# A gated mix of linear attention and a ReLU layer: weight loads merged, value tiles moved forward, the last two tiles split in halves

## The chip, the cores and the metric

The kernel runs on one core of a Trainium2 chip. The core has several engines that run their own instruction queues and wait for one another by semaphores: TensorE (PE: matmuls, and PEld: the load of the stationary operand), VectorE (DVE), ScalarE (ACT), GpSimd (POOL) and SyncE (SP), which here only issues DMAs. The metric is the device time of one execution in microseconds (us); the figure given is the median of several runs.

## The reference, cut to what matters

Sizes: 2048 tokens, D = 512, 32 heads of 16 columns, a hidden layer of 1376 columns, all in bf16. Two branches read the same x and are mixed by a gate per token.

```python
g = sigmoid((x * gate_w).sum(-1, keepdims=True))
q, k, v = heads(x @ wqkv)                      # 32 heads of 16
pq, pk  = q @ w_phi[h], k @ w_phi[h]           # 16 x 16 per head
phi     = lambda t: concat(softmax(t), softmax(-t))
kv, z   = sum_s phi(pk) v, sum_s phi(pk)       # over all tokens
o       = (phi(pq) @ kv) / (phi(pq) . z + 1e-6)
a       = o @ wo
b       = relu(x @ w1) @ w2
out     = g * a + (1 - g) * b
```

## The kernel before, in words

The instructions of each engine are recorded by hand in the order in which the program is written: p.op adds one to an engine's queue with the events it waits for, p.dma does the same for a DMA, and emit turns events into semaphore waits. So the order of the source is the order of each queue. An engine takes its instructions strictly in order: one that waits holds up all that follow.

Tokens are worked on in 16 tiles of 128 (index m) and 4 chunks of 512 (index c). x is kept transposed in XT. The accumulators of TensorE are the 8 banks of PS. `free[bank]` names the event (an eviction by ScalarE or VectorE) after which a bank may be written again.

The stages, in order:

- **Loads** (L164 to L189, on SyncE): W1 in pieces, part of x, the rest of W1, w_phi, the value weights WV, then two transposing loads of the query and the key columns of wqkv (L185) into WQKT (a corner of PHQ), then chunks 1 to 3 of x, transposing (L188).
- **Slabs** (L518): eight 128-column blocks of the hidden layer for chunk 0, contraction slab by contraction slab; slab 3 waits for the load of W1's fourth row block (w13). Then hidden units (0, 8) and (0, 9), which also need the right-hand columns of W1.
- **Value tiles** (vtile, L401 to L414): four matmuls x @ wv into a bank (2, unless another is named), copied out to VS.
- **Folds** (pre, L300 to L313): the query and key weights are multiplied with w_phi, so that pq and pk come from x in one matmul. Eight of them, 0 to 3 for the query, 4 to 7 for the key; four matmuls each into banks 0, 1, 6, 7 in turn; even ones are copied out by VectorE, odd ones by ScalarE. Only 15 of 16 columns a head are computed, the 16th being a constant.
- **Ragged unit** (rest, L279 to L297): the last 96 columns of the hidden layer and the gate column for one chunk, token-major, evicted by two ScalarE instructions and transposed by a DMA.
- **The loop over tiles** (L574): atile(m) computes pq and pk of tile m (8 matmuls into banks 0 and 1), takes exponentials of both signs on ScalarE (two instructions over both banks, or four where m is in split), then the key chain (sum on VectorE, reciprocal, scaling into EB slot 3, on GpSimd except for tile 15) and the query chain (qchain, ending in a transposing DMA to PHQ). Behind atile(m) stand kv(m - 3), which adds tile m - 3 to the accumulators of kv in banks 6 and 7, vtile(m + 3), and the hidden units listed in mid[m] (hunit, L269: four matmuls and a relu eviction on ScalarE).
- **Hand-over** (L589 on): the remaining hidden units in late, with kv(13), kv(14), kv(15) and kvfin (VectorE masks kv into KVNZ) between them, then nd(0), qchain(15), the gate, finB(0, 4).
- **The output stage** (L608): per tile nd (phi(pq) @ kv, into banks 0 and 1 or 2 and 3), finB (hidden layer @ w2, eleven matmuls at L483), finA (@ wo), and comb, which mixes and stores.

Hidden units, ragged units and one value tile take their bank from a rotation over banks 3, 4 and 5:

```python
def nextbank():
    rot[0] += 1
    return 3 + (rot[0] - 1) % 3
```

finB(0, 4) names bank 4, and its first matmul waits for whatever eviction last freed that bank.

Of the kernel before, what the change touches and what calls it, by code (L numbers as in the profile page):

```python
# [68 lines left out]
def bass_gated_mix__linear_kernel_hedgehog__dense_activation_relu__prompt_kernel(  # L69
# [13 lines left out]
    S, D = x2.shape  # L83
# [3 lines left out]
    P = 128  # L87
# [17 lines left out]
    with ExitStack() as es:  # L105
# [55 lines left out]
        def loadw1(t, c0=0, c1=DFF, tag=""):  # L161
            p.dma("sp", lambda e: e.dma_start(  # L162
                out=W1[:, t, c0:c1], in_=B_w1[t * P:(t + 1) * P, c0:c1]), f"w1{t}{tag}", ev=f"w1{t}{tag}")
# [6 lines left out]
        p.early("sp")  # L170
        loadw1(0, 0, 4 * P, "a")
        loadw1(0, 4 * P, 8 * P)
        for t in (1, 2):
            loadw1(t, 0, 8 * P)
        p.dma("sp", lambda e: e.dma_start_transpose(  # L175
            out=XT[:, 2:4, 0:512], in_=x2[0:512, 2 * P:4 * P]), "x0t", ev="x0t")
        loadw1(3, 0, 8 * P)
        p.dma("sp", lambda e: e.dma_start(
            out=W1[:, :, 8 * P:DFF], in_=B_w1[:, 8 * P:DFF].rearrange("(j p) n -> p j n", p=P)), "w1r", ev="w1r")
        p.dma("sp", lambda e: e.dma_start(  # L180
            out=WPS[:, :, :], in_=A_w_phi.rearrange("(g hl) r c -> (hl r) g c", g=NDT)), "wps", ev="wps")
        p.dma("sp", lambda e: e.dma_start(  # L182
            out=WV[:, :, :], in_=A_wqkv[:, 2 * D:3 * D].rearrange("(j p) n -> p j n", p=P)), "wv", ev="wv")
        for i in range(2):
            p.dma("sp", lambda e, i=i: e.dma_start_transpose(  # L185
                out=WQKT[:, 4 * i:4 * i + 4, :], in_=A_wqkv[:, i * D:(i + 1) * D]), f"wqk{i}", ev=f"wqk{i}")
        for c in range(1, NCH):
            p.dma("sp", lambda e, c=c: e.dma_start_transpose(  # L188
                out=XT[:, :, c * 512:(c + 1) * 512], in_=x2[c * 512:(c + 1) * 512, :]), f"x{c}", ev=f"x{c}")  # L189
# [75 lines left out]
# [3 lines that stand above are left out]
# [32 lines left out]
        def pre(i):  # L300
            which, dt = i // 4, i % 4
            bank = (0, 1, 6, 7)[i % 4]
            dst = WQK[:, which, dt * DE:(dt + 1) * DE]
            after = [f"wqk{which}"] + [f"wbd{g}" for g in range(NDT)] + free[bank]
            for gt in range(NDT):
                p.op("pe", lambda e, gt=gt: e.matmul(  # L306
                    PS[:, bank, gt * 8 * FE:(gt + 1) * 8 * FE], WQKT[:, which * NDT + gt, dt * P:(dt + 1) * P],
                    Wbd[:, gt, :], start=True, stop=True),
                    after=(after if gt == 0 else ()), ev=(f"pm{i}" if gt == NDT - 1 else None))
            if i % 2 == 0:  # L310
                p.op("dve", lambda e: e.tensor_copy(dst, PS[:, bank, 0:DE]), after=[f"pm{i}"], ev=f"pc{i}")
            else:
                p.op("act", lambda e: e.activation(dst, PS[:, bank, 0:DE], ACT.Copy),  # L313
                     after=[f"pm{i}"], ev=f"pc{i}")
            free[bank] = [f"pc{i}"]

        split = (5, 8, 11, 13, 14, 15)

        def atile(m):
            b = m % NB  # L320
            first = xready(m // 4)
            order = [(dt, w) for dt in range(NDT) for w in range(2)]
            if m - 1 in split:
                order = [(dt, w) for w in (1, 0) for dt in range(NDT)]
            if m == 0:
                order = [(dt, w) for w in (0, 1) for dt in range(NDT)]
            for i, (dt, which) in enumerate(order):
                p.op("pe", lambda e, dt=dt, which=which: e.matmul(  # L328
                    PS[:, which, 0:DE], XT[:, dt, m * P:(m + 1) * P], WQK[:, which, dt * DE:(dt + 1) * DE],
                    start=(dt == 0), stop=(dt == NDT - 1)),  # L330
                    after=(first if i == 0 else []) + (free[which] if dt == 0 else [])
                    + ([f"pc{4 * which + c}" for c in range(4)] if m == 0 and dt == 0 else []),
                    ev=(f"qk{m}" if i == 7 else None))
            src = PS[:, 0:2, 0:DE].rearrange("p a (h f) -> p a h f", h=H)
            base = b * 8 * D
            busy = [f"tq{m - NB}", f"pk{m - NB}", f"pq{m - NB}"] if m >= NB else []

            def expo(s, w, ev):
                step = (4 * D, 2 * D)[s]
                off = base + s * (2 * D + 16)  # L340
                scale = (1.0, -1.0)[s]
                if w is None:
                    dst = bass.AP(tensor=EB, offset=off, ap=[[EBS, P], [step, 2], [32, H], [1, FE]])
                    s_ = src
                else:
                    dst = bass.AP(tensor=EB, offset=off + w * step, ap=[[EBS, P], [32, H], [1, FE]])
                    s_ = src[:, w, :, :]
                p.op("act", lambda e: e.activation(dst, s_, ACT.Exp, scale=scale),  # L348
                     after=[f"qk{m}"] + busy, ev=ev)

            if m in split:
                for w, nm in ((1, "k"), (0, "")):
                    expo(0, w, f"ep{nm}{m}")
                    expo(1, w, f"em{nm}{m}")
            else:
                expo(0, None, f"ep{m}")
                expo(1, None, f"em{m}")
            emk = f"emk{m}" if m in split else f"em{m}"
            free[1] = [emk]
            free[0] = [f"em{m}"]  # L360
            zk = ZB[:, b, 64:128].rearrange("p (h s) -> p h s", s=2)
            ek = EB[:, b, 2, :].rearrange("p (h s f) -> p h s f", h=H, s=2)
            if m == NT - 1:
                for s, nm in ((0, "epk"), (1, "emk")):
                    p.op("dve", lambda e, s=s: e.tensor_reduce(zk[:, :, s], ek[:, :, s, :], AX.X, ALU.add),
                         after=[f"{nm}{m}", f"cst{b}"], ev=f"zk{m}" if s else None)
            else:
                p.op("dve", lambda e: e.tensor_reduce(zk, ek, AX.X, ALU.add),  # L368
                     after=[emk, f"cst{b}"], ev=f"zk{m}")
            p.op("dve", lambda e: e.reciprocal(SC[:, b, 64:128], ZB[:, b, 64:128]),  # L370
                 after=[f"zk{m}"] + ([f"pk{m - NB}"] if m >= NB else []), ev=f"rz{m}")
            p.op("pool" if m < NT - 1 else "dve", lambda e: e.tensor_tensor(  # L372
                EB[:, b, 3, :].rearrange("p (g f) -> p g f", f=DH),
                EB[:, b, 2, :].rearrange("p (g f) -> p g f", f=DH),
                SC[:, b, 64:128].unsqueeze(2).to_broadcast([P, 2 * H, DH]), ALU.mult),
                after=[f"rz{m}"] + ([f"kv{m - NB}"] if m >= NB else []), ev=f"pk{m}")
            if m < NT - 1:
                qchain(m)

        def qchain(m):  # L380
            b = m % NB
# [172 lines left out]
        gatecol(0)  # L554
        vtile(0, "dve")
        vtile(1, "act", nextbank())
        for i in range(4):
            pre(i)
        vtile(2, "dve")
        for i in range(4, 8):  # L560
            pre(i)
        rest(0)
        mid = [[(1, 0), (1, 1)], [(1, 2), (1, 3)], [(1, 4), (1, 5)], [(1, 6), (1, 7)], [(1, 8), (1, 9)], [(2, 0)],
               [(1, -1), (2, 1)], [(2, 2), (2, 3)], [(2, 4)], [(2, -1), (2, 5)], [(2, 6), (2, 7)], [(2, 8)],
               [(3, -1), (2, 9)], [(3, 0), (3, 1)], [(3, 2), (3, 3)], []]
        late = [(3, k) for k in range(4, KU)]

        def unit(c, k):
            if k < 0:
# [1 line left out]
            else:  # L571
                hunit(c, k)

        for m in range(NT):  # L574
            atile(m)
            if m >= LAG:
                kv(m - LAG)
            if m + 3 < NT:
                vtile(m + 3)
            for u in mid[m]:  # L580
                unit(*u)
            if m == 3:
                for a, b in ((0, 5), (5, KU)):
                    p.dma("sp", lambda e, a=a, b=b: e.dma_start(
                        out=W2[:, a:b, :], in_=B_w2[a * P:b * P, :].rearrange("(j p) n -> p j n", p=P)),
                        "w2", ev=f"w2{a}")
                p.dma("sp", lambda e: e.dma_start(out=W2[0:NR, KU, :], in_=B_w2[KU * P:DFF, :]), "w2", ev="w2")
            if m == 5:
                for a in range(0, NDT, 2):  # L589
                    p.dma("sp", lambda e, a=a: e.dma_start(  # L590
                        out=WO[:, a:a + 2, :], in_=A_wo[a * P:(a + 2) * P, :].rearrange("(j p) n -> p j n", p=P)),
                        "wo", ev="wo" if a else None)
        for i, u in enumerate(late):
            if i == 0:
                kv(NT - 3)
            if i == 2:
                kv(NT - 2)
            if i == 4:
                kv(NT - 1)
                kvfin()  # L600
            unit(*u)
        nd(0)
        qchain(NT - 1)
        gate()
# [57 lines left out]
```

## Time and profile before

| what | us |
|---|---|
| median of 3 runs | 147.15 (146.97 to 147.18) |
| span of the profiled execution | 146.3 |
| TensorE busy | 143.0 |
| VectorE busy | 91.7 |
| ScalarE busy | 72.4 |
| GpSimd busy | 52.2 |
| issue of the first transposing weight load, on SyncE | 5.77 |
| issue of the second | 2.25 |
| first lands, second lands (from the span's start) | 15.25, 17.53 |

The profile is of one execution; its span runs from its first to its last instruction, and the measured time of a run is some 0.85 us longer than that span. All times in the profile are counted from the span's start. In a line of the timeline the columns are start, duration, engine, source line, operation, output <- inputs, shapes and number of instructions, and in brackets the idle time of the engine before it with what ended it. PHQ<-in_A_wqkv_dram is the transposing weight load, since WQKT lies in PHQ. In the table by windows each entry is the busy time of an engine in the window and its number of instructions; the last two columns are the mean share of the DMA engines and GB/s. The granted TensorE clock is 1.00 in every window.

### The profile page before, as it was taken

Reading aid. Unit: us, or ns where it says so; the run is one execution under the profiler, and the core shown is the slowest. Engines: PE = TensorE matmul, PEld = TensorE weight load, DVE = VectorE, ACT = ScalarE, POOL = GpSimd, SP = SyncE. Lnnn points to the kernel's source line nnn. Section 1 sums busy time; section 2 is a strip of 40 time slices with the busy share of each in tenths; the row PEclk is TensorE's granted clock in tenths of the full one; section 3 lists DMA queues with packets and bytes.
Section 4 is the critical chain, followed back from the end, with each engine's and each line's share of the span. In section 5 each row is a group of like instructions: output and inputs, shape, how many; then the busy total and the mean of one; then the engine's idle time right before and its main releaser. Section 6 shows DMA issues by size and latency. Waiting matters only on the chain.

```text
span 146.3 us, 2520 instructions
## 1 busy us (share of the span) xinstructions
PE 143.0 (98%) x970; PEld 72.3 (49%) x970; DVE 91.7 (63%) x156; ACT 72.4 (49%) x124; POOL 52.2 (36%) x62
## 2 busy tenths in 40 slices
PE   8999799999999999999999999999999999999994
PEld 3444564444455545544645555554444444444443
DVE  4338627777687878678698977674445555555342
ACT  4134467798778778887878862022221111111150
POOL 2013002778768678688869820300000000000000
DMA  5998998033549984335333431354333223222213
GB/s 150 262 276 163 231 167 186 3 69 72 76 80 328 179 201 73 72 72 108 78 72 75 104 72 31 81 108 117 85 82 78 72 72 76 72 72 74 72 44 106
DMA packets 46517, 16.12 MB, mean 110 GB/s; under 512 B 40392, under 2 KB 46120, under 8 KB 46504
## 3 DMA queue, kind: packets, MB, share of 16 engines
q1 hardware_dynamic: 46352, 15.92, 50.3%
q8 instruction: 8, 0.13, 0.4%
q10 hardware_dynamic: 152, 0.03, 0.1%
q14 instruction: 5, 0.04, 0.1%
HBM read 4.15 MB, written 2.10 MB: 43 GB/s over the span
## 4 chain that ended last, share of the span: by engine, by line
PE 86%; SPq 7%; DMA 4%; DVE 1%; issue 0%
PE PS L483 26%; PE PS L328 18%; PE PS L272 18%; PE PS L492 9%; PE PS L404 8%; SPq L185 4%; DMA PHQ<-in_A_wqkv_dram 4%; PE PS L458 3%; PE PS L426 3%; PE PS L284 2%; SPq L162 2%; SPq L175 1%; PE PS L306 1%; DVE WQK L506 1%; SPq L182 0%
## 5 line engine op out<-in xcount | busy, mean ns | idle before, releaser
L483 PE MATMUL PS<-W,HT 128*128 128x512 bf16 (+4 forms) x187 | 40.6, 366 | 0.0
L372 POOL TENSOR_TENSOR EB<-EB,SC 128x1024 bf16<-128x1024 bf16 x15 | 28.9, 1930 | 23.4 <-DVE SC L370 23.4
L348 ACT ACTIVATE EB<-PS 128x480 bf16<-128x480 f32 (+1 forms) x44 | 30.1, 756 | 14.2 <-PE PS L328 14.2
L497 ACT ACTIVATE TFA<-PS,GT 128x512 bf16<-128x512 f32 x16 | 11.0, 687 | 42.7 <-PE PS L492 36.6
L272 PE MATMUL PS<-XT,W 128*128 128x512 bf16 x128 | 30.7, 379 | 0.0
L328 PE MATMUL PS<-WQK,XT 128*128 128x480 bf16 x128 | 28.5, 366 | 0.0
L368 DVE TENSOR_REDUCE ZB<-EB 128x64 f32<-128x1024 bf16 x15 | 18.3, 1220 | 14.7 <-ACT EB L348 14.7
L506 DVE SCALAR_TENSOR_TENSOR WQK<-PS,OMG,TFA 128x512 bf16<-128x512 f32 (+2 forms) x17 | 12.2, 719 | 23.6 <-ACT TFA L497 22.4
L483 PEld LDWEIGHTS PS<-W,HT 128*128 128x128 bf16 (+1 forms) x187 | 17.0, 98 | 17.4
L258 ACT ACTIVATE HT<-PS 128x512 bf16<-128x512 f32 x35 | 20.3, 614 | 7.4 <-PE PS L520 5.6
L328 PEld LDWEIGHTS PS<-WQK,XT 128*128 128x128 bf16 x128 | 12.5, 98 | 13.6
L383 DVE TENSOR_REDUCE ZB<-EB 128x64 f32<-128x1024 bf16 x16 | 18.6, 1164 | 0.0
L272 PEld LDWEIGHTS PS<-XT,W 128*128 128x128 bf16 x128 | 12.0, 98 | 13.2
L392 POOL TENSOR_TENSOR EB<-EB,SC 128x512 bf16<-128x512 bf16 x16 | 16.9, 1059 | 1.3
L404 PE MATMUL PS<-WV,XT 128*128 128x512 bf16 x64 | 16.2, 378 | 0.0
L492 PE MATMUL PS<-WO,OT 128*128 128x512 bf16 x64 | 16.1, 378 | 0.0
L468 DVE TENSOR_TENSOR WQK<-PS,RDEN 128x512 bf16<-128x512 f32 x16 | 11.1, 692 | 0.5
L492 PEld LDWEIGHTS PS<-WO,OT 128*128 128x128 bf16 x64 | 6.1, 97 | 7.2
L414 ACT ACTIVATE VS<-PS 128x512 bf16<-128x512 f32 x14 | 8.5, 608 | 2.0 <-PE PS L404 2.0
L370 DVE RECIPROCAL SC<-ZB 128x64 f32<-128x64 f32 x16 | 8.8, 553 | 0.5
L458 PEld LDWEIGHTS PS<-KVNZ,PHQ 128*128 128x128 bf16 x128 | 6.1, 97 | 3.6
L404 PEld LDWEIGHTS PS<-WV,XT 128*128 128x128 bf16 x64 | 5.4, 97 | 4.8
(57 smaller groups left out, 85.7 us busy)
## 6 DMA issues: line engine op xcount, KB each, us to landing
out_dram<-WQK SPq DMA_DIRECT2D x15, 128.0 KB, 1.7
W<-in_B_w_dram SPq DMA_DIRECT2D x2, 640.0 KB, 5.8
W<-in_B_w_dram SPq DMA_DIRECT2D x3, 256.0 KB, 3.8
WV<-in_A_wqkv_dram SPq DMA_DIRECT2D x1, 512.0 KB, 6.5
WO<-in_A_wo_dram SPq DMA_DIRECT2D x2, 256.0 KB, 3.0
W<-in_B_w_dram SPq DMA_DIRECT2D x1, 352.0 KB, 5.1
OT<-in_A_x_dram SPq DMA_DIRECT2D x2, 128.0 KB, 2.3
W<-in_B_w_dram SPq DMA_DIRECT2D x2, 128.0 KB, 3.0
```

Of the source, the lines that this page charges most:

```text
L258: p.op("act", lambda e: e.activation(dst, src, ACT.Relu), after=[f"h{c}_{kt}"], ev=ev)
L272: p.op("pe", lambda e, t=t: e.matmul(PS[:, bank, :], W1[:, t, kt * P:(kt + 1) * P], XT[:, t, c * 512:(c + 1) * 512], start=(t == 0), stop= ...
L328: p.op("pe", lambda e, dt=dt, which=which: e.matmul(PS[:, which, 0:DE], XT[:, dt, m * P:(m + 1) * P], WQK[:, which, dt * DE:(dt + 1) * DE] ...
L348: p.op("act", lambda e: e.activation(dst, s_, ACT.Exp, scale=scale), after=[f"qk{m}"] + busy, ev=ev)
L368: p.op("dve", lambda e: e.tensor_reduce(zk, ek, AX.X, ALU.add), after=[emk, f"cst{b}"], ev=f"zk{m}")
L372: p.op("pool" if m < NT - 1 else "dve", lambda e: e.tensor_tensor(EB[:, b, 3, :].rearrange("p (g f) -> p g f", f=DH), EB[:, b, 2, :].rearr ...
L383: p.op("dve", lambda e: e.tensor_reduce(ZB[:, b, 0:64].rearrange("p (h s) -> p h s", s=2), bass.AP(tensor=EB, offset=base, ap=[[EBS, P], [ ...
L392: p.op("pool", lambda e: e.tensor_tensor(EB[:, b, 0, :].rearrange("p (h s f) -> p h s f", h=H, s=2)[:, :, 1, :], EB[:, b, 1, :].rearrange( ...
L404: p.op("pe", lambda e, dt=dt: e.matmul(PS[:, bank, :], XT[:, dt, m * P:(m + 1) * P], WV[:, dt, :], start=(dt == 0), stop=(dt == NDT - 1)), ...
L483: p.op("pe", lambda e, kt=kt, M=M: e.matmul(PS[:, bank, 0:n], HT[0:M, kt, m * P:(m + 1) * P], W2[0:M, kt, cs], start=(kt == 0), stop=(kt = ...
L492: p.op("pe", lambda e, t=t: e.matmul(PS[:, bank, :], OT[:, t, m * P:(m + 1) * P], WO[:, t, :], start=(t == 0), stop=(t == NDT - 1)), after ...
L506: p.op("dve", lambda e: e.scalar_tensor_tensor(out=OSB[:, ob, cs], in0=PS[:, bank, 0:n], scalar=OMG[:, m:m + 1], in1=TFA[:, m % 2, cs], op ...
```

## The change

It edits five things. The two transposing loads of the query and key weights become one, of 1024 columns, with one event, wqk. Value tiles 2 and 3 are computed before the folds, tile 3 with a bank from the rotation; the loop's first pass has no value tile, and three hidden units. The ragged unit of chunk 0 moves between folds 0 to 3 and folds 4 to 7. W1's fourth row block is loaded whole (1376 columns), and the load of the right-hand columns covers three row blocks only. The loop ends at tile 13; tiles 14 and 15 are done in halves, key half before query half (new function half), interleaved with units (3, 3) to (3, 6) and the last kv; atile's key chain becomes a function of its own, kchain, and mid is dealt out anew, one unit earlier for each tile.

```diff
-        for t in (1, 2):
-            loadw1(t, 0, 8 * P)
+        loadw1(1, 0, 8 * P)
+        loadw1(2, 0, 8 * P)
...
-        loadw1(3, 0, 8 * P)
+        loadw1(3)
         p.dma("sp", lambda e: e.dma_start(
-            out=W1[:, :, 8 * P:DFF], in_=B_w1[:, 8 * P:DFF].rearrange("(j p) n -> p j n", p=P)), "w1r", ev="w1r")
+            out=W1[:, 0:3, 8 * P:DFF], in_=B_w1[0:3 * P, 8 * P:DFF].rearrange("(j p) n -> p j n", p=P)),
+            "w1r", ev="w1r")
...
-        for i in range(2):
-            p.dma("sp", lambda e, i=i: e.dma_start_transpose(
-                out=WQKT[:, 4 * i:4 * i + 4, :], in_=A_wqkv[:, i * D:(i + 1) * D]), f"wqk{i}", ev=f"wqk{i}")
+        p.dma("sp", lambda e: e.dma_start_transpose(out=WQKT[:, :, :], in_=A_wqkv[:, 0:2 * D]), "wqk", ev="wqk")
...
-            after = [f"wqk{which}"] + [f"wbd{g}" for g in range(NDT)] + free[bank]
+            after = ["wqk"] + [f"wbd{g}" for g in range(NDT)] + free[bank]
...
-        split = (5, 8, 11, 13, 14, 15)
+        split = (5, 8, 11, 13)
...
+            kchain(m, emk)
+            qchain(m)
+
+        def half(m, w, bank):
+            b = m % NB
+            nm = ("", "k")[w]
+            for dt in range(NDT):
+                p.op("pe", lambda e, dt=dt: e.matmul(
+                    PS[:, bank, 0:DE], XT[:, dt, m * P:(m + 1) * P], WQK[:, w, dt * DE:(dt + 1) * DE],
+                    start=(dt == 0), stop=(dt == NDT - 1)),
+                    after=(xready(m // 4) + free[bank] if dt == 0 else ()), ev=(f"l{w}{m}" if dt == NDT - 1 else None))
+            for s in range(2):
+                dst = bass.AP(tensor=EB, offset=b * 8 * D + s * (2 * D + 16) + w * (4 * D, 2 * D)[s],
+                              ap=[[EBS, P], [32, H], [1, FE]])
+                p.op("act", lambda e, s=s, dst=dst: e.activation(
+                    dst, PS[:, bank, 0:DE].rearrange("p (h f) -> p h f", h=H), ACT.Exp, scale=(1.0, -1.0)[s]),
+                    after=[f"l{w}{m}", f"tq{m - NB}", f"pk{m - NB}", f"pq{m - NB}"], ev=f"e{'pm'[s]}{nm}{m}")
+            free[bank] = [f"em{nm}{m}"]
+
+        def kchain(m, emk):
+            b = m % NB
...
-            if m < NT - 1:
-                qchain(m)
...
         vtile(1, "act", nextbank())
+        vtile(2, "dve")
+        vtile(3, "act", nextbank())
         for i in range(4):
             pre(i)
-        vtile(2, "dve")
+        rest(0)
         for i in range(4, 8):
             pre(i)
-        rest(0)
-        mid = [[(1, 0), (1, 1)], [(1, 2), (1, 3)], [(1, 4), (1, 5)], [(1, 6), (1, 7)], [(1, 8), (1, 9)], [(2, 0)],
-               [(1, -1), (2, 1)], [(2, 2), (2, 3)], [(2, 4)], [(2, -1), (2, 5)], [(2, 6), (2, 7)], [(2, 8)],
-               [(3, -1), (2, 9)], [(3, 0), (3, 1)], [(3, 2), (3, 3)], []]
-        late = [(3, k) for k in range(4, KU)]
+        mid = [[(1, 0), (1, 1), (1, 2)], [(1, 3), (1, 4)], [(1, 5), (1, 6)], [(1, 7), (1, 8)], [(1, 9), (2, 0)], [(2, 1)],
+               [(1, -1), (2, 2)], [(2, 3), (2, 4)], [(2, 5)], [(2, -1), (2, 6)], [(2, 7), (2, 8)], [(2, 9)],
+               [(3, -1), (3, 0)], [(3, 1), (3, 2)]]
...
-        for m in range(NT):
+        for m in range(NT - 2):
             atile(m)
             if m >= LAG:
                 kv(m - LAG)
-            if m + 3 < NT:
+            if 0 < m and m + 3 < NT:
                 vtile(m + 3)
...
-        for i, u in enumerate(late):
-            if i == 0:
-                kv(NT - 3)
-            if i == 2:
-                kv(NT - 2)
-            if i == 4:
-                kv(NT - 1)
-                kvfin()
-            unit(*u)
+        half(NT - 2, 1, 1)
+        kv(NT - 5)
+        kchain(NT - 2, f"emk{NT - 2}")
+        unit(3, 3)
+        half(NT - 1, 1, 0)
+        kchain(NT - 1, f"emk{NT - 1}")
+        unit(3, 4)
+        half(NT - 2, 0, 1)
+        qchain(NT - 2)
+        kv(NT - 4)
+        unit(3, 5)
+        half(NT - 1, 0, 0)
+        kv(NT - 3)
+        kv(NT - 2)
+        unit(3, 6)
+        kv(NT - 1)
+        kvfin()
+        for k in range(7, KU):
+            unit(3, k)
```

## The prediction

> **What bounds the kernel now.** I read first the busy shares, then the chain of waits.
>
> ```profile
> PE 143.0 (98%) x970; PEld 72.3 (49%) x970; DVE 91.7 (63%) x156; ACT 72.4 (49%) x124; POOL 52.2 (36%) x62
> ```
>
> TensorE is busy for 143.0 of 146.3 us; no other engine is above 63%. So only two things can move the end: matmul work (the change adds and removes none), or places where TensorE stands still. The chain, in order of time, shows where that is; columns are start, duration, what.
>
> ```profile
> 6.60 5.77 SPq L185
> 12.36 0.04 issue
> 12.41 5.12 DMA PHQ<-in_A_wqkv_dram
> 17.53 0.04 issue
> 17.57 1.01 PE PS L306 x16
> ...
> 143.75 0.62 DVE WQK L506
> ```
>
> Between 17.57 and 143.73 every step of the chain is a matmul. The chain enters TensorE through the second transposing load of the query and key weights, which lands at 17.53. The timeline of TensorE around that point shows what it does meanwhile:
>
> ```profile
> 12.89 1.89 PE L404 MATMUL PS<-WV,XT 128*128 128x512 bf16 x8
> 15.30 1.01 PE L306 MATMUL PS<-Wbd,PHQ 128*128 128x120 bf16 x16 [0.52 <-DMA PHQ<-in_A_wqkv_dram]
> 16.15 1.03 PE L404 MATMUL PS<-WV,XT 128*128 128x512 bf16 x4
> 17.57 1.01 PE L306 MATMUL PS<-Wbd,PHQ 128*128 128x120 bf16 x16 [0.40 <-DMA PHQ<-in_A_wqkv_dram]
> 18.42 0.86 PE L284 MATMUL PS<-W,XT 128*128 128x97 bf16 x16
> ```
>
> Two waits, one for each load. A group's duration includes the draining of its last matmul, so I count by first matmuls: four value matmuls step in 0.86 (0.216 each, from the chain), a fold group in 0.85 (15.30 to 16.15), the ragged unit in 0.70 (18.42 to 19.12, where query/key tile 0 starts). From 12.89 to 19.12 there is work for 3 x 0.86 + 2 x 0.85 + 0.70 = 4.98 in 6.23 us: 1.25 us lost. This is all that the change can win.
>
> **The fold, after.** Value tiles 0 to 3 run first. Tile 2 needs the bank of tile 0, whose copy on VectorE (13.95, 0.69) ends at 14.64, against 12.89 + 1.73 = 14.62: with 0.05 for the semaphore, 0.07 lost. So the value tiles are through at 12.89 + 3.46 + 0.07 = 16.42. Then TensorE waits for the one load; call its landing L, first matmul at L + 0.04 (17.53 to 17.57 before). Then folds 0 to 3 (0.85), ragged unit (0.70), folds 4 to 7. Here a cover is gone: the ragged unit stood between the last folds and tile 0, and tile 0 writes bank 0, which fold 4's copy frees. In the trace that copy ends 1.08 after its group starts (17.57; copies at 17.99, 0.65 each), so tile 0 starts 1.08 + 0.05 = 1.13 after, not 0.85. Its key half comes 0.81 later, at 1.94; the copies it needs sit on ScalarE behind the ragged unit's two evictions and end at about 1.75 (rows L291 0.49, L293 0.17, L313 0.57): hidden. Tile 0 starts at L + 0.04 + 0.85 + 0.70 + 1.13 = L + 2.72. Before, it started at 19.12 with value tile 3 (0.86) still to do, so compare with 19.98. The difference is L - 17.26.
>
> **L.** No row has a 512 x 1024 transposing load. Bounds from the neighbours: SyncE's issue of the second 512 x 512 load took 2.25, of an x chunk of the same size 2.20, of the 512 x 256 part of x 1.33, so another 512 columns cost 1.75 to 2.25. The first took 5.77: 3.5 of it stood still until 12.36, when the value weights were about to land (6.05 + 6.5 = 12.55); I expect the same hold-up. The single issue then ends at 12.36 + 1.75 = 14.1 to 14.6. From end of issue to landing the weights took 2.87 (17.53 - 14.66), the x chunks down to 2.06 (5.2 - 3.14): L is between 16.2 and 17.5. The DMA's own rate decides where:
>
> ```profile
> 12.40:13.80 1.40, 1.40 (x9) 0.66 (x8) 0.86 (x3) 0.40 (x1) 0.00 (x0) 1.00 1.21 271
> 13.80:15.20 1.40, 0.98 (x5) 0.25 (x3) 0.73 (x2) 0.39 (x1) 0.00 (x0) 1.00 0.85 124
> 15.20:16.40 1.20, 1.10 (x18) 0.99 (x19) 0.68 (x2) 0.69 (x3) 0.00 (x0) 1.00 1.25 277
> ```
>
> (Last column GB/s; the one before, mean share of the 16 DMA engines.) Between the two loads the rate falls to 124 for 1.4 us. At 271 the same bytes pass in 0.64, so the seam costs 0.76. One load has no seam: L = 17.53 - 0.76 = 16.77. I take that; it lies just above the middle of the bounds. The fold then gives 16.77 - 17.26 = -0.49 us.
>
> [...]
>
> **A bank that changes hands.** The diff does not say this. Value tile 3 used bank 2; now it takes one from the rotation of banks 3, 4, 5 (L265), so each later unit is one bank on. Before, 37 draws are made and the last, unit (3, 9), gets bank 3; now there are 38, and it gets bank 4. finB(0, 4), the first group of the last stage, writes bank 4. Before, it waited for the eviction of unit (3, 7), long done; now for that of (3, 9), with only nd(0) in between. The rows of before (TensorE, and the last eviction on ScalarE):
>
> ```profile
> 86.48 1.89 PE L272 MATMUL PS<-XT,W 128*128 128x512 bf16 x8
> 88.20 0.42 PE L458 MATMUL PS<-KVNZ,PHQ 128*128 128x68 bf16 x8
> 88.46 2.54 PE L483 MATMUL PS<-W,HT 128*128 128x512 bf16 x11
> ...
> 88.40 0.60 ACT L258 ACTIVATE HT<-PS 128x512 bf16<-128x512 f32 x1 [0.27 <-PE PS L272]
> ```
>
> finB(0) starts at 88.46; the eviction ends at 89.00. With the semaphore it would start at 89.06: +0.60 us. Everything to the end is queued behind it on TensorE, so all of it counts. The 35 rows of this eviction run from 0.59 to 0.64, which bounds the wait at 0.59 to 0.64; 0 only if it is not there at all.
>
> **The last two tiles** cost nothing if their key chains keep up. On the clock of before, tile 13 ends at 75.00; adding chain rows (kv 0.25, unit 0.86, half tile 0.81), kv(14) starts at 83.55 and kv(15) at 84.66. For kv(14): GpSimd ends tile 13 at 80.21 + 1.06 = 81.27, then 1.93, so 83.20: 0.35 to spare. For kv(15): VectorE is free at 79.03 + 0.35; then 1.22 + 0.55 (tile 14), 1.22 + 0.55 + 1.23 (tile 15) end at 84.2: 0.5 to spare. They give nothing either, as before had no stall there; without the slack each costs what it is late. kvfin waits for VectorE's query sums of tile 14 until about 85.6 and ends at about 86.7; nd(0) needs it at 88.2. The same units per tile stand between the other tiles, so banks 0 and 1 come free as before.
>
> **W1's last slab whole** makes that load 352 KB instead of 256. It was issued at 4.41 and such loads land within 3.9, so by 8.3; slab 3 needs it eight matmuls before the hidden units start at 11.14, at 9.4; 96 KB more at the 262 GB/s of that slice of the page is 0.4 us: hidden, 0.7 to spare. The rest of W1 is smaller by the same bytes, so what follows lands as before. The x chunks are issued after the one load, about 0.1 to 0.5 earlier, and are needed later: nothing.
>
> **Sum.** -0.49 + 0.60 = +0.11 us on the profiled execution of 146.3. The runs' median is 147.15, 0.85 above the span; I add the difference to the median: 147.26, said as 147.25. In general the sum is L - 16.66, and it cannot fall below -0.28, as the value tiles end at 16.42.
>
> **Rivals.** (1) Slower: the single load is no quicker than the pair, the pause being DMA work and not a seam; nothing starts until all of it has landed. L = 17.53: +0.87, 148.0. It decides from L = 16.95 on. For it: both weight loads took 2.87 from end of issue to landing, and 14.6 + 2.87 is 17.5. Against: the x chunks after them had 2.5 and less. (2) Faster: the bank wait is not there and the fold gives its share: 147.15 - 0.49 = 146.65. For it: the eviction is one of 35 and ScalarE idles before it; against: its start is bound to the end of the last unit, and no matmul but nd(0) is between. (3) The key chain of tile 14 or 15 is late: halves put four more waits on ScalarE's order; 0.7 us more work than I count on VectorE or GpSimd would cost 0.2 to 0.35: 147.55. (4) The single load lands before 16.4: then the floor, 146.87, which differs from no change by hardly more than the measurement can tell.
>
> **Chances.** A measurement of this kernel can tell about 0.2%, 0.29 us, from no change. Forecast (L from 16.4 to 16.95, bank wait paid): 0.48, no change that can be told. Rival 1: 0.32. Rival 3: 0.08. Rivals 2 and 4 together: 0.12. So faster 0.12, same 0.48, slower 0.40. The range is 146.8 (just under the floor) to 147.95 (rival 1 nearly whole); the likeliest case alone spans 146.9 to 147.45.
>
> **What would show it.** One wait in front of the first fold group, of 0.2 to 0.5 us, in place of two; tile 0's first matmul 0.28 late behind fold 4's copy; a gap of about 0.4 to 0.6 ahead of the first L483 group (its new line number), released by ScalarE's relu; none between tiles 13 and 15. Wrong would be a landing after 17.0 or before 16.4, no gap at finB(0), or gaps at kv(14) or kv(15).

## The result, and the profile after

| | us |
|---|---|
| changed, median of 14 runs | 147.62 (147.03 to 148.26) |
| before, median of 14 runs in the same rounds | 147.06 (146.18 to 147.25) |
| ratio | 1.0048, 95% interval 1.0032 to 1.0064 |
| span of the profiled execution, changed | 145.8 |

The changed kernel is slower by 0.5%. A second set of runs gave 1.007 (1.0045 to 1.0095). Yet its profiled execution has a shorter span than that of before (146.3). Each of the 14 runs is listed with its own span, about 1.3 us below its time (1.2 to 1.4; the 0.85 given with the profile before set one execution against the median of other runs). The profiled 145.8 belongs to 147.07, the second lowest of the 14. By the same step the 146.3 of before would be about 147.6, above every one of its 14 runs. Both profiles are from the edges of their spread, in opposite directions, which has to be kept in mind when they are read against each other.

The chain of waits of the changed kernel, from the first value tile to query/key tile 0 (start, duration, what):

```profile
12.67 3.57 PE PS L422 x16
16.24 0.84 PE PS L305 x16
17.08 0.69 PE PS L283 x16
17.77 0.22 PE PS L305 x4
18.00 0.02 issue
18.02 0.67 DVE WQK L310
18.69 0.05 issue
18.73 1.79 PE PS L327 x8
```

No load is in it: value tiles run into folds, folds into the ragged unit. The one load was issued at 6.58 and landed 8.9 later, at 15.5, while the fourth value tile was still running. What stands ahead of tile 0 (L327) is fold 4's copy on VectorE (L310).

The same view where the last stage begins:

```profile
84.54 2.60 PE PS L271 x12
87.15 0.02 issue
87.17 0.61 ACT HT L257
87.78 0.14 issue
87.91 2.54 PE PS L501 x11
```

The last hidden units end at 87.15, ScalarE evicts the last one, and only then does finB(0) (L501) begin. In the timeline nd(0)'s first matmul is at 86.97, so it is 0.94 from there to finB(0); before it was 88.20 to 88.46, 0.26. So 0.68 us is lost. Between tile 13 and this point the chain is matmuls back to back, as it is from finB(0) to the last one. From tile 0 to nd(0) the changed kernel takes 68.24 (18.73 to 86.97); with the 0.86 of value tile 3, which it has done ahead of tile 0, that is 69.10, and before it was 69.08 (19.12 to 88.20). So the loop and the tail cost the same in both, and behind the first value matmul what differs lies at the fold and at finB(0).

### The profile page after: what moved, and what is told of

Same layout as the page of the kernel before. It is cut to its first block, busy times and chain, and to the rows that moved or that the text cites. A ratio compares the mean times of both kernels' runs of the same rounds, so it can differ in the third digit from the quotient of the medians.

```text
span 145.8 us, 2516 instructions
## 1 busy us (share of the span) xinstructions
PE 142.7 (98%) x970; PEld 72.3 (50%) x970; DVE 91.8 (63%) x156; ACT 72.6 (50%) x124; POOL 52.0 (36%) x62
## 4 chain that ended last, share of the span: by engine, by line
PE 97%; DVE 1%; ACT 0%; issue 0%; DVEq 0%
PE PS L501 26%; PE PS L271 19%; PE PS L327 16%; PE PS L422 10%; PE PS L510 9%; PE PS L538 5%; PE PS L444 3%; PE PS L476 3%; PE PS L367 2%; PE PS L283 2%; PE PS L230 2%; PE PS L305 1%; PE PS L236 1%; DVE WQK L524 1%; DVE WQK L310 0%; ACT HT L257 0%
## 5 line engine op out<-in xcount | busy, mean ns | idle before, releaser
L501 PE MATMUL PS<-W,HT 128*128 128x512 bf16 (+4 forms) x187 | 40.6, 366 | 0.5 <-ACT HT L257 0.5
L347 ACT ACTIVATE EB<-PS 128x960 bf16<-128x960 f32 (+1 forms) x36 | 26.2, 796 | 13.1 <-PE PS L327 13.1
L501 PEld LDWEIGHTS PS<-W,HT 128*128 128x128 bf16 (+1 forms) x187 | 17.0, 98 | 18.0 <-issue 0.6
L327 PE MATMUL PS<-WQK,XT 128*128 128x480 bf16 x112 | 25.0, 366 | 0.1
L327 PEld LDWEIGHTS PS<-WQK,XT 128*128 128x128 bf16 x112 | 10.9, 98 | 12.2 <-DVE WQK L310 0.3
L482 DVE RECIPROCAL RDEN<-PS 128x32 f32<-128x32 f32 x16 | 5.6, 350 | 4.0 <-PE PS L476 4.0
```

What stands on the lines that cost most here:

```text
L327: p.op("pe", lambda e, dt=dt, which=which: e.matmul(PS[:, which, 0:DE], XT[:, dt, m * P:(m + 1) * P], WQK[:, which, dt * DE:(dt + 1) * DE] ...
L501: p.op("pe", lambda e, kt=kt, M=M: e.matmul(PS[:, bank, 0:n], HT[0:M, kt, m * P:(m + 1) * P], W2[0:M, kt, cs], start=(kt == 0), stop=(kt = ...
```

## The experiments

All ratios are to the kernel before, run on the same chip in the same rounds. "Lost at the fold" is what I measure in each profile: from the first value matmul to the first matmul of tile 0, less the work in between (4.98 us with three value tiles, as in the prediction; 5.84 with a fourth of 0.86).

**1. The changed kernel again.**

> The changed kernel as it is, for a second profile and more times. Theory A (the bank that finB(0) now shares with the last unit costs 0.6 us, and the fold gives little in a usual run): 0.4 to 0.7 us over the kernel before, a gap of 0.5 us ahead of finB(0), and, since the profile had the load landing at 15.5 with no wait for it while its time was among the lowest of 14, a landing that differs from profile to profile, between 15.4 and 17.5. Rival R (the one load is late as a rule and makes the whole loss): a landing of 17 or later here. Rival S (nothing of either; the times only scatter): within 0.2 us of the kernel before.

1.007 (1.0045 to 1.0095), median 148.04 of 6 runs; span 146.8. The load landed at 16.08, again with no wait for it; lost at the fold 0.37 (0.36 in the first profile); finB(0) 0.95 after nd(0). That is 1.1 us over the kernel before by the medians and 0.7 to 1.4 by the ratio, where theory A said 0.4 to 0.7: its upper edge and above. From its first value matmul to the end the execution took 133.3, as did the first profile (133.3): the 1 us between the two spans lies in the first 13 us, and has no part in the change's own stages.

**2. The bank put back.** Value tile 3 takes bank 4 by name, so the rotation is drawn 37 times as before.

```diff
-        vtile(3, "act", nextbank())
+        vtile(3, "act", 4)
```

> The changed kernel with value tile 3 on bank 4 by name, so that the rotation is drawn 37 times as before and unit (3, 9) gets bank 3. Theory A: the gap ahead of finB(0) goes and the time falls by 0.5 to 0.6 us against the changed kernel, to about the time before or up to 0.3 us below it. Rival R: the gap goes from the profile but the time stays within 0.2 us of the changed kernel. Rival S: no difference.

1.0015 (0.9994 to 1.0036), 147.10. The gap has gone. The median is 0.9 us below that of experiment 1 (six runs), more than theory A's 0.5 to 0.6, and not below the kernel before. TensorE's timeline:

```profile
85.15 2.75 PE L271 MATMUL PS<-XT,W 128*128 128x512 bf16 x12
87.73 0.42 PE L476 MATMUL PS<-KVNZ,PHQ 128*128 128x68 bf16 x8
87.99 2.54 PE L501 MATMUL PS<-W,HT 128*128 128x512 bf16 x11
```

nd(0) to finB(0) is 0.26 again, and most of the slowdown is gone with it. From the first value matmul to the end: 132.6, against 133.3.

**3. Two loads again**, everything else as changed.

```diff
-        p.dma("sp", lambda e: e.dma_start_transpose(out=WQKT[:, :, :], in_=A_wqkv[:, 0:2 * D]), "wqk", ev="wqk")
+        for i in range(2):
+            p.dma("sp", lambda e, i=i: e.dma_start_transpose(
+                out=WQKT[:, 4 * i:4 * i + 4, :], in_=A_wqkv[:, i * D:(i + 1) * D]), f"wqk{i}", ev=f"wqk{i}")
...
-            after = ["wqk"] + [f"wbd{g}" for g in range(NDT)] + free[bank]
+            after = [f"wqk{which}"] + [f"wbd{g}" for g in range(NDT)] + free[bank]
```

> The changed kernel with the two transposing loads of 512 columns each, each fold waiting for its own; all else as changed. Theory A, by the trace of before: the first load lands at 15.25, hidden by the value tiles to 16.4, the second at 17.53, when folds 0 to 3 and the ragged unit end at 18.0: no wait for either, so 0.3 to 0.6 us faster than the changed kernel in usual runs if the one load is late there, and no different if it lands by 16.4 as in its profile. Rival R: faster by 0.5 us or more. Rival S: no difference.

1.0063 (1.0038 to 1.0088), 147.83: no different from the changed kernel. The loads landed at 14.39 and 16.71, the fold groups started at 16.13 and 17.66, waiting for neither. With four value tiles ahead, one load or two makes no difference that these runs can tell. That rules out rival R, by which the one load made the loss.

**4. W1 as before**, everything else as changed.

```diff
-        loadw1(3)
+        loadw1(3, 0, 8 * P)
...
-            out=W1[:, 0:3, 8 * P:DFF], in_=B_w1[0:3 * P, 8 * P:DFF].rearrange("(j p) n -> p j n", p=P)),
+            out=W1[:, :, 8 * P:DFF], in_=B_w1[:, 8 * P:DFF].rearrange("(j p) n -> p j n", p=P)),
```

> The changed kernel with W1 loaded as before (fourth row block in two parts). Theory A: within 0.15 us of the changed kernel, as the larger load lands before slab 3 needs it. Rival T (the whole row block delays slab 3, or the loads behind it): faster than the changed kernel by 0.3 us or more. The slabs ended 0.2 us earlier in the profile after than in that before, which speaks against T, or for a gain: then this one is slower by 0.2 to 0.4 us.

1.0048 (1.0028 to 1.0069), 147.53. The ratio is that of the first set of the changed kernel, 1.0048; against the set of the same rounds (experiment 1, 1.007, six runs) it is 0.3 us lower by the ratios and 0.5 by the medians, with intervals that overlap. So theory T is neither borne out nor ruled out by the times.

**5. The kernel before again.**

> The kernel before, once more, for a second profile. The profiled span of before, 146.3, is above most spans of its timed runs (144.9 to 146.0 where listed). Theory A2 (the waits of 0.5 and 0.4 us ahead of the folds are from a slow execution; in a usual one the weights land earlier and the waits are smaller): span 145.0 to 146.0, the second weight load landing before 17.2, and less than 0.6 us lost between the value tiles and query/key tile 0, against 1.25. Rival (before always pays the 1.25 us, and its executions differ only in the first 5 us, by the number of matmuls that take 0.43 us): 1.1 to 1.3 lost there again, and a faster start.

1.0005 (0.9988 to 1.0023). Span 145.7. TensorE's timeline:

```profile
13.08 1.89 PE L404 MATMUL PS<-WV,XT 128*128 128x512 bf16 x8
14.80 1.00 PE L306 MATMUL PS<-Wbd,PHQ 128*128 128x120 bf16 x16
15.64 1.03 PE L404 MATMUL PS<-WV,XT 128*128 128x512 bf16 x4
17.00 1.01 PE L306 MATMUL PS<-Wbd,PHQ 128*128 128x120 bf16 x16 [0.33 <-DMA PHQ<-in_A_wqkv_dram]
17.85 0.86 PE L284 MATMUL PS<-W,XT 128*128 128x97 bf16 x16
18.54 1.78 PE L328 MATMUL PS<-WQK,XT 128*128 128x480 bf16 x8
```

One wait in place of two: the loads landed at 14.34 and 16.95 and the first was not waited for. 18.54 - 13.08 - 4.98 = 0.48 us lost, where the profile I predicted from lost 1.25. Theory A2 holds.

**6. One draw more in the kernel before.** A bank is drawn and not used. Every unit of the loop is then one bank on, as in the change; only the output stage names one of these banks itself.

```diff
         late = [(3, k) for k in range(4, KU)]
+        nextbank()
```

> The kernel before with one bank drawn from the rotation and not used, ahead of the loop, so that unit (3, 9) gets bank 4, as in the changed kernel; nothing else. Theory A: 0.6 to 0.7 us slower than before (0.4 to 0.5%), with one new gap of about 0.5 us ahead of finB(0). Rival (the change's loss lies in its tail halves or its fold): within 0.2 us of before.

1.0051 (1.0032 to 1.007), 147.62: a slowdown as large as that of the change, from one bank number. From tile 0 to nd(0) it takes 69.08, as before, so the loop itself is untouched. The chain has the same two steps as in the changed kernel:

```profile
88.13 0.61 ACT HT L258
88.74 0.14 issue
88.87 2.54 PE PS L483 x11
```

nd(0) starts at 87.93, finB(0) 0.94 later. The fold shows something else. TensorE's timeline of this execution:

```profile
13.89 1.89 PE L404 MATMUL PS<-WV,XT 128*128 128x512 bf16 x8
15.61 1.00 PE L306 MATMUL PS<-Wbd,PHQ 128*128 128x120 bf16 x16
16.45 1.03 PE L404 MATMUL PS<-WV,XT 128*128 128x512 bf16 x4
17.31 1.00 PE L306 MATMUL PS<-Wbd,PHQ 128*128 128x120 bf16 x16
18.15 0.86 PE L284 MATMUL PS<-W,XT 128*128 128x97 bf16 x16
18.85 1.38 PE L328 MATMUL PS<-WQK,XT 128*128 128x480 bf16 x6
```

No wait at all, and with tile 0 at 18.85 it is 18.85 - 13.89 = 4.96, nothing lost. The loads landed at 14.28 and 16.81, much as in the execution of experiment 5, but TensorE came 0.81 us later, and tile 0 only 0.31 later. So in the kernel before, a late start of TensorE is made good in part at the fold: 0.5 of 0.8 here, and no more than what is lost there otherwise.

**7. The ragged unit behind all folds** (bank put back).

```diff
         for i in range(4):
             pre(i)
-        rest(0)
         for i in range(4, 8):
             pre(i)
+        rest(0)
```

> The changed kernel with value tile 3 on bank 4 by name and the ragged unit behind all eight folds, as it stood before. In the profiles of the changed kernel query/key tile 0 starts 1.12 after folds 4 to 7 start, behind fold 4's copy, where the matmuls alone take 0.85; the ragged unit would cover that. Theory A: 0.25 to 0.3 us faster than the kernel with the bank put back alone, 146.75 or so, and no gap ahead of tile 0. Rival (without the ragged unit between them the later folds wait for the copies of the earlier ones, or tile 0's start moves the wait elsewhere): within 0.1 us of it.

1.0035 (1.0015 to 1.0055), 147.36: not faster than with the bank put back alone (1.0015 and, in experiment 11, 1.003), as the rival had it. TensorE's timeline:

```profile
16.95 2.28 PE L305 MATMUL PS<-Wbd,PHQ 128*128 128x120 bf16 x32
19.07 0.86 PE L283 MATMUL PS<-W,XT 128*128 128x97 bf16 x16
```

The eight folds step in 2.12, where two groups take 1.70: folds 4 to 7 write the banks of folds 0 to 3 and wait for their copies. 0.42 is paid there and 0.28 saved ahead of tile 0. By the profile the position of the ragged unit between the groups is the better one, by 0.14; the times can't tell that.

**8. The old tail** (bank put back): tiles 14 and 15 whole, as before, on the changed front.

```diff
-        split = (5, 8, 11, 13)
+        split = (5, 8, 11, 13, 14, 15)
...
-               [(3, -1), (3, 0)], [(3, 1), (3, 2)]]
+               [(3, -1), (3, 0)], [(3, 1), (3, 2)], [(3, 3), (3, 4)], []]
+        late = [(3, k) for k in range(5, KU)]
...
-        for m in range(NT - 2):
+        for m in range(NT):
...
-        half(NT - 2, 1, 1)
...
+        for i, u in enumerate(late):
+            if i == 0:
+                kv(NT - 3)
+            if i == 1:
+                kv(NT - 2)
+            if i == 3:
+                kv(NT - 1)
+                kvfin()
+            unit(*u)
```

> The changed kernel with value tile 3 on bank 4 by name and tiles 14 and 15 whole, as before (units dealt out as in the change up to tile 13, then two after tile 14, the other five behind tile 15 with kv(13), kv(14), kv(15) between). Theory A (the halves neither cost nor gain): within 0.15 us of the kernel with the bank put back alone. Rival U (the halves cost what was left of 0.2 us in that one): 0.2 us faster than it or more.

1.007 (1.0044 to 1.0097), 147.89: slower, neither theory. TensorE's timeline:

```profile
82.86 1.02 PE L271 MATMUL PS<-XT,W 128*128 128x512 bf16 x4
83.91 0.42 PE L445 MATMUL PS<-VS,EB 128*128 128x65 bf16 x8
84.17 1.89 PE L271 MATMUL PS<-XT,W 128*128 128x512 bf16 x8
86.35 0.42 PE L445 MATMUL PS<-VS,EB 128*128 128x65 bf16 x8 [0.30 <-DVE EB L393]
```

By first matmuls kv(14) comes 83.91 - 82.86 - 0.86 = 0.19 late, as GpSimd's scaling of tile 14 ends at 83.85, and kv(15) 86.35 - 84.17 - 1.73 = 0.45 late, waiting for VectorE's scaling of tile 15. That sum, 0.64, is what this kernel takes longer, to 0.03, from its first value matmul to the end (133.3 against 132.6 in experiment 2). The unit spent at the front is missing here as cover: kv(14) and kv(15) each have one unit fewer ahead of them than before. So with that unit gone, and the kv placed as here, whole tiles put the key chains on the path, and the halves of the change keep them off it.

**9 and 10. Bank waits taken away, twice.** Value tile 2 on bank 3, tile 3 on bank 4, folds 4 and 5 in banks 2 and 5, which tile 0 does not write (folds 6 and 7 stay in 6 and 7).

```diff
-            bank = (0, 1, 6, 7)[i % 4]
+            bank = (0, 1, 6, 7, 2, 5, 6, 7)[i]
...
-        vtile(2, "dve")
-        vtile(3, "act", nextbank())
+        vtile(2, "dve", 3)
+        vtile(3, "act", 4)
```

> The changed kernel with its bank waits taken away: value tile 2 on bank 3 and tile 3 on bank 4 by name (rotation as before), folds 4 to 7 into banks 2, 5, 6, 7 in place of 0, 1, 6, 7, so that query/key tile 0 doesn't wait for fold 4's copy. Theory A: no gap ahead of finB(0); from the first value matmul to tile 0 (four value tiles, eight folds, ragged unit) 5.85 to 6.0 us, where the changed kernel took 6.20; 0.2 to 0.35 us faster than the bank put back alone, so 0.0 to 0.4 us below the kernel before. Rival V (the key half of tile 0 then waits for folds 5 and 7 on ScalarE as long as tile 0 waited before): 6.1 or more from value to the second half of tile 0, and no faster than the bank put back alone.

> The same kernel as the one before it in this list, for twice as many times. Theory A: as there, and both intervals cover the same figure. If the two differ by more than 0.3 us, differences of that size can't be told in this study.

1.0015 (0.9995 to 1.0035) and 0.9988 (0.997 to 1.0006), medians 146.93 and 146.56. TensorE's timeline of the second:

```profile
13.00 3.61 PE L422 MATMUL PS<-WV,XT 128*128 128x512 bf16 x16
16.45 1.00 PE L305 MATMUL PS<-Wbd,PHQ 128*128 128x120 bf16 x16
17.29 0.86 PE L283 MATMUL PS<-W,XT 128*128 128x97 bf16 x16
17.98 1.00 PE L305 MATMUL PS<-Wbd,PHQ 128*128 128x120 bf16 x16
18.82 1.91 PE L327 MATMUL PS<-WQK,XT 128*128 128x480 bf16 x8
```

18.82 - 13.00 = 5.82: the fold is free of loss. The eight matmuls of tile 0 take 1.91 where they took 1.79, so 0.12 of rival V's wait is there, and no more. In time, the same kernel came out 0.37 us apart in its two sets. By the expectation's own rule a difference of that size can't be told here: this kernel is level with the one before, and whether it beats it stays open.

**11. The bank put back, once more.**

> The changed kernel with value tile 3 on bank 4 by name once more, for more times. Theory A: 0.0 to 0.3 us above the kernel before, 0.5 to 0.7 below the changed one. Rival W (the fold of the changed kernel is no better than before even with the load early): 0.3 us or more above the kernel before.

1.003 (1.0014 to 1.0046), 147.11, and 0.37 lost at the fold. That is 0.3 us above the kernel before by the medians and 0.4 by the ratio, where theory A ends and rival W begins: in time, this fold is no better than that of before. With experiment 2 (whose interval takes in no change), the rest of the change, without its bank, comes out 0.15 to 0.3% slower than before, not faster.

**12. The one load alone**, in the kernel before (its edit is that of experiment 3 backwards).

> The kernel before with the one load of 1024 columns alone; value tiles, ragged unit, W1 and tail as before. In the profiles so far the one load lands 4.0 to 4.4 after the value weights, the second of two 4.9 to 5.4, the first of two 2.4 to 2.8. Theory A: all folds now wait for 4.0 to 4.4, the first up to 1.6 longer than before, the second group no more; folds 0 to 3 start at 15.6 to 16.8 with a wait of 0.5 to 1.5 us ahead of them and none ahead of folds 4 to 7; 0.1 to 0.5 us slower than before. Rival R2 (the single load is what gains, wherever the value tiles stand): 0.2 us or more faster than before.

1.0067 (1.0043 to 1.0091), 147.83. TensorE's timeline:

```profile
13.40 1.89 PE L402 MATMUL PS<-WV,XT 128*128 128x512 bf16 x8
16.58 1.01 PE L304 MATMUL PS<-Wbd,PHQ 128*128 128x120 bf16 x16 [1.30 <-DMA PHQ<-in_A_wqkv_dram]
17.43 1.03 PE L402 MATMUL PS<-WV,XT 128*128 128x512 bf16 x4
18.30 1.00 PE L304 MATMUL PS<-Wbd,PHQ 128*128 128x120 bf16 x16
19.14 0.86 PE L282 MATMUL PS<-W,XT 128*128 128x97 bf16 x16
19.83 1.38 PE L326 MATMUL PS<-WQK,XT 128*128 128x480 bf16 x6
```

One wait of 1.30, ahead of folds 0 to 3; 1.45 lost at the fold (19.83 - 13.40 - 4.98). The waits are theory A's; the time is not, 1.0 us slower (0.6 to 1.3 by the ratio) where it said 0.1 to 0.5. Rival R2, a gain, is ruled out. Counted from the landing of the value weights, the one load took 4.4 here, where the first of two took 2.4 to 2.8 and the second 4.9 to 5.4: it is later for the first folds by more than it is early for the last. It needs the value tiles ahead of it; they don't need it (experiment 3).

## Why the prediction came out as it did

I forecast 147.25, no change that can be told, with 0.40 on slower; 147.62 is inside the range, on its slower side. By the prediction's own measure, 0.2%, the measured 0.5% is a slowdown that can be told, and most of the 0.40 was for rival (1), a late load, which no run showed. That the time lies so near the forecast is in part luck: two errors cancelled in part. Point by point:

- **The bank that changes hands: right, and the main cause.** Experiment 6 puts it alone into the kernel before and gets a slowdown as large as the change's; experiment 2 takes it out of the changed kernel and most of it goes. Its size was put at 0.60 and is 0.68 or 0.69 in all five profiles that have it (0.94 or 0.95 from nd(0) to finB(0), less 0.26): from the end of the eviction to the first matmul it takes 0.13 us, where I allowed 0.06.
- **The 1.25 us lost at the fold before: mis-sized.** "This is all that the change can win" was read from one execution, whose span puts it above all 14 timed runs. Three profiles of before's fold (the first, experiments 5 and 6) lost 1.25, 0.48 and nothing. Which it is depends on TensorE's start against the loads: the value tiles began at 12.89, 13.08 and 13.89, the second load landed at 17.53, 16.95 and 16.81.
- **L = 16.77: too late.** In the nine profiles with the one load and four value tiles it landed between 15.5 and 16.8, and it ended TensorE's wait in none but one (experiment 4, 16.82, folds at 16.87). From the landing of the value weights it took 3.9 to 4.4, the second of two loads 4.9 to 5.4: about 1 us between them, where I took 0.76 for the seam. But 16.77 is 4.23 after the value weights, which landed at 12.54 in that execution, so the time of the load itself was well put. What made L late is the execution: in the 14 profiles the value weights landed between 11.5 and 12.6, in most of them before 12.0.
- **The two errors cancelled in part.** The win at the fold was counted against a slow execution of before, and L was taken from the same one. The floor that I worked out, the value tiles' own end, gave -0.88 at the fold against the profiled execution; the changed profile against it is 0.36 - 1.25 = -0.89. Against the mean of the three executions of before, 0.58, it is -0.22. With 0.68 for the bank that makes +0.46 us; measured +0.5% (0.7 us, interval 0.5 to 0.9) and once 0.7%. The sum of the record, -0.49 + 0.60, was 0.35 below this. Without the first execution the other two of before lost 0.24 on the mean, and the sum is +0.80. What is left between sum and measurement can't be told from the choice of executions.
- **Tile 0 behind fold 4's copy: right.** Worked out as 1.13 after the group's start, measured 17.61 to 18.73, 1.12. The wait of value tile 2 was 0.07, measured 0.08 (3.54 for sixteen matmuls that step in 3.46). Both show as the 0.36 lost, and both go in experiments 9 and 10.
- **The tail: right that it costs nothing as changed**, by the gapless chain and the 69.10 against 69.08. The slack was smaller than I counted: in the changed profile GpSimd ends tile 14's scaling at 82.78 and kv(14) starts at 83.02, VectorE ends tile 15's at 83.87 and kv(15) starts at 84.13, so 0.24 and 0.26 were to spare where I had 0.35 and 0.5. In experiment 8, with whole tiles and one unit less of cover, there was none.
- **W1's last slab whole: not shown to matter.** Experiment 4 leaves it open. The transposing load of x ahead of it landed at 7.4 to 7.7 in the five profiles with W1 as before, and at 7.2 to 8.2 in the nine with the whole slab, and slab 2 waits for it. Those means are 0.2 us apart, 7.5 and 7.7. Against a loss speaks that the first value matmul, behind all slabs, came at 13.30 on the mean in the five and at 13.15 in the nine. With such a spread neither settles it.
- **Two readings that were wrong.** Against rival (1) I had the x chunks landing 2.5 us and less after the end of their issue; the second of the three took 3.5 (16.94 + 2.21 to 22.64), so that argument was weaker than it looked. And 16.77 lies just below the middle of the bounds 16.2 to 17.5, not above it. Neither changed the sum.

Of the rivals, (1) (the one load no quicker than the pair) is ruled out by the landings, none of them after 16.82; (2) (the bank wait not there) by the gap; (3) (late key chains) did not happen in the changed kernel; (4) (the load before 16.4) is what usually happened, but was priced against an execution that was slow for the kernel before.

## What to carry to other kernels

A helper that hands out buffers in turn couples places that are far apart: one more draw at the front moved the last unit onto the bank that the next stage names, and cost 0.5% where the rest of the change won nothing that could be told. Count the draws, or name the buffers at a hand-over. And where a wait for a load is read from one execution, a second profile of the same kernel tells whether it is a property of the kernel or of that execution: here 1.25, 0.48 and 0 us.

## What the runs showed of the hardware that was not expected

**TensorE's first matmuls are slow for a varying time.** At the start of the slabs 128x512 matmuls step in 0.43 us in some executions until 5.9 and later, in others in 0.22 from the first. Matmuls of the slabs by window, for experiment 1 and then experiment 7 (from:to, length, TensorE busy and number of matmuls, weight loads, granted clock, DMA share, GB/s):

```profile
3.80:4.80 1.00, 0.90 (x3) 0.38 (x4) 1.00 0.91 316
4.80:5.80 1.00, 1.00 (x4) 0.29 (x3) 1.00 1.28 280
5.80:6.80 1.00, 1.00 (x6) 0.40 (x5) 1.00 0.78 131
```

```profile
3.80:4.80 1.00, 1.00 (x6) 0.37 (x6) 1.00 1.02 346
4.80:5.80 1.00, 1.00 (x6) 0.39 (x5) 1.00 1.13 311
5.80:6.80 1.00, 1.00 (x7) 0.41 (x5) 1.00 1.63 157
```

Three and four matmuls in a microsecond in the one, six in the other, with a granted clock of 1.00 in both. In the 14 profiles the first step of 0.22 in the slabs comes between 3.7 and 6.7. What makes the steps ahead of it longer, and what ends them, no run shows.

**An early start need not help.** In experiment 7, whose matmuls were fast from the first, the chain goes through the transposing load of x instead:

```profile
3.02 5.04 DMA XT<-in_A_x_dram
8.06 0.14 issue
8.20 3.61 PE PS L538 x16
```

It landed at 8.06, and slab 2 stood for 0.99 us. Slow matmuls at the start, this load and the weight loads at the fold each set the pace in some executions. In the two profiles of the changed kernel the whole scatter of 1 us lies ahead of the first value matmul, and it is larger than most single steps of the change.
